# Maximum scores of two tiles in row halves of TensorE, ahead of the value products

## The chip, the cores and the metric

The kernel runs on one core of a Trainium2 chip. The metric is the device time of one execution in microseconds (us). The engines of a core run their own programs in order and wait for each other by semaphores: TensorE (PE; its weight loads are listed as PEld), VectorE (DVE), ScalarE (ACT), GpSimd (POOL) and SyncE (SP, which issues DMAs).

## The reference

Attention with normalised queries and keys (batch 8, 12 heads, 448 positions, head size 64), and behind it a mixture of eight experts with one expert a token. What the change touches is the attention:

```python
q_n, k_n = (rmsnorm(q, g_q), rmsnorm(k, g_k))
scores = scale * np.matmul(q_n, k_n.transpose(0, 1, 3, 2))
scores = scores - np.max(scores, axis=-1, keepdims=True)
attn = np.exp(scores)
attn = attn / (np.sum(attn, axis=-1, keepdims=True) + 1e-09)
return np.matmul(attn, v).astype(np.float32)
```

The maximum of a row of scores only shifts numerator and denominator of the softmax by a common factor, so it may come from less exact scores than the ones that are exponentiated.

## The kernel before

Attention goes by units: unit u is two heads of one batch entry, 48 units in all. The two heads' 896 positions make seven tiles of 128 (j = 0 to 6; tile 3 has the last 64 positions of the first head and the first 64 of the second). A unit takes seven steps; step number n = 7 i + j in the code, for n from -22 to 335. In step n TensorE makes the transposed scores of unit i, tile j (`st`, L944: a first product with 128 rows, and a second with 65, whose last row subtracts the maximum), ACT exponentiates them, and the work of other units is put around it by a plan that is written out before the loop (L1223 to L1275, from the table `PLAN`). The loop over n (L1276 on) emits each step's instructions engine by engine, so the order in the loop is the order in each engine's program. The parts that matter here:

- `tr` (L829): transposes of the normalised q or k of a unit into a PSUM tile of pool `ps_t`, which has two buffers. From it come the rounded copy `h_`, which is `hi_b[u % 2][g]` (q for g = 0, k for g = 1; the first head in partitions 0 to 63, the second in 64 to 127), and the remainder `l_` that the rounding left (function `dve`, on DVE, the last reader of the tile). DMAs move halves of both into `qq`, `kk`, `ql` and `kh`, which stack a rounded part and a remainder in 128 rows.
- `sa` (L908): scores of unit u, tile j with positions of q as rows, into one of the two buffers of pool `ps_a`; DVE reduces them to one maximum a row (`t["mx"]`). Except for unit 0 and tile 3 it multiplies `qq` by `kk`, 128 rows. For unit 0 it multiplies the rounded copies of the tile's head, 64 rows. Tile 3 multiplies the rounded copies over 128 rows with the other head's places zeroed.
- `mt` (L931): a transpose of the seven maxima of a unit into a `ps_t` buffer; ACT copies it and a DMA puts it into row 64 of `ql`.
- `av` (L982): the value products. For c = 0 to 2 they use 64 of the array's columns for each head (twelve instructions a unit, as each product of full precision is two); for c = 3, once in two units, 64 rows and 64 columns.
- `sums` (L1004), `psums` (L1013) and `gates` (L1022): products into 32 columns each (tile pm). `recips` (L1034): transposes `sp` into a `ps_t` buffer, once in four units, at step 6 behind the transposes of k.

In steady state the plan has `sa` of unit u, tile j at n = 7 u - 14 + j: each step has one `sa`, of the unit two ahead of the one in `st`. `mt` of unit u stands at n = 7 u - 6 and the value products of c = 0 to 2 at n = 7 i + 1 or so: both in step 1. The transposes of k come in step 6, those of q in step 2. In a step TensorE's order is `st`, `sa`, `tr`, `mt`, `recips`, then `av`, `sums`, `gates`. Units below 10 have times of their own in `PLAN["first"]`, and units 1 to 6 a shorter distance between their `sa` (`sastep`).

Of the kernel before, what the change touches and what calls it, by code (L numbers as in the profile page):

```python
# [69 lines left out]
def kernel(  # L70
# [660 lines left out]
    if True:  # L731
        zt = view(yw, 0, 128, NE * NT * 2 // 128)
# [543 lines left out]
        for n in range(P["start"], NJ * NU):  # L1276
            i, j = divmod(n, NJ)
# [372 lines left out]
```

## Time and profile before

| | |
|---|---|
| median of 3 runs | 1020.1 us (1019.49 to 1020.82) |
| the profiled execution | 1020.89 us, its span 1019.1 us |
| mean granted TensorE clock | 0.992 of full speed |
| PE busy | 990.7 us (97%), 5731 instructions |
| DVE, ACT, POOL busy | 797.5, 733.4, 712.9 us |
| attention stage | until some 530 us, the experts from there on |

The span is that of the instructions on the engines; the execution's time has a little around it. Busy time of matmuls is modelled (they are pipelined), so it says less than the order in which they start. Times of instructions are counted from the span's start.

### The profile page before, as it was taken

The page shows a single profiled execution, that of the slowest core. Times are in us where ns is not written, and L with a number is a line of the kernel's source. Part 1 is how long each engine was busy: PE and PEld are TensorE (multiplying, and loading weights), DVE is VectorE, ACT ScalarE, POOL GpSimd, SP SyncE. Part 2 cuts the span into 40 slices and gives each one's busy share as a digit, 9 for nine tenths or more (in the row PEclk, how much of TensorE's full clock was granted, in tenths as well). Part 3 has the DMA queues.
Part 4 walks back from the last instruction along what each step waited for, and adds up shares of the span by engine and source line. Part 5 has one row for each costly group of instructions (what it writes and reads, how often), then busy time and mean ns, then how long its engine had stood idle before and what let it go on. Part 6 is the DMA issues. An engine that isn't in the chain of part 4 may idle for free.

```text
span 1019.1 us, 18323 instructions
## 1 busy us (share of the span) xinstructions
PE 990.7 (97%) x5731; PEld 763.2 (75%) x5731; DVE 797.5 (78%) x1560; ACT 733.4 (72%) x1576; POOL 712.9 (70%) x732
## 2 busy tenths in 40 slices
PE   8999999999999999999999999999999999999996
PEld 6755656565666655555549999989999999999986
DVE  7898888887888888988569988767877777777760
ACT  8798989988989889887565566556656665666550
POOL 5767777988888989798876767566555765566141
PEclk8999999999999999999999999999999999999998
DMA  7777777777877777765753122112171211121070
GB/s 193 177 201 195 195 182 184 185 173 180 197 178 192 179 178 178 190 142 128 200 170 88 50 37 75 36 49 64 48 279 49 64 50 36 43 63 48 16 282 35
DMA packets 174430, 132.77 MB, mean 130 GB/s; under 512 B 119039, under 2 KB 168035, under 8 KB 173172
## 3 DMA queue, kind: packets, MB, share of 16 engines
q1 hardware_dynamic: 149844, 90.21, 36.8%
q0 software_dynamic: 23856, 41.28, 12.5%
q8 instruction: 47, 0.77, 0.3%
q14 instruction: 59, 0.48, 0.2%
q10 hardware_dynamic: 624, 0.02, 0.0%
HBM read 139.06 MB, written 23.72 MB: 160 GB/s over the span
## 4 chain that ended last, share of the span: by engine, by line
PE 87%; ACT 4%; DVE 4%; DMA 2%; issue 2%; POOL 1%; SPq 0%; POOLq 0%; DVEq 0%; ACTq 0%
PE py L610 23%; PE st L950 15%; PE av L994 12%; PE sa L923 5%; PE tr L836 3%; PE ph_2a L579 3%; PE ph_3s L579 2%; PE ph_0a L579 2%; PE ph_3a L579 2%; PE ph_1s L579 2%; PE ph_0s L579 2%; PE ph_1a L579 2%; PE ph_2s L579 2%; PE pm L1009 2%; DVE at_hlw L55 1%
## 5 line engine op out<-in xcount | busy, mean ns | idle before, releaser
L55 DVE TENSOR_REDUCE at_hlw<-sa 128x1 f32<-128x448 f32 x336 | 203.6, 612 | 63.8 <-PE sa L923 50.7
L950 PE MATMUL st<-w1w 128*128 128x448 f32 x480 | 174.1, 411 | 6.9 <-ACT at_w2lw L55 5.4
L55 POOL DMA_INDIRECT xrw<-x_d,i x112 | 133.5, 1192 | 33.4 <-issue 31.7
L950 PEld LDWEIGHTS st<-w1w 128*128 128x128 f32 x480 | 83.3, 189 | 97.9 <-ACT xw L55 25.6
L55 POOL DMA_INDIRECT r2w<-in_moe_w_dram,tb_w2i x48 | 50.4, 1050 | 106.0 <-DVE w2lw L55 97.3
L55 DVE TENSOR_TENSOR w1w<-r,w1w 128x512 fp32r<-128x512 f32 (+1 forms) x180 | 107.0, 644 | 14.8 <-ACT w1w L55 14.6
L55 ACT ACTIVATE at_w2lw<-st 128x448 f32<-128x448 f32 x168 | 90.0, 540 | 35.7 <-PE st L950 33.1
L610 PE MATMUL py<-w2lw,hhw 128*128 128x384 f32 x448 | 115.2, 334 | 0.0
L55 ACT CAST w1w<-xw 64x448 fp32r<-64x448 f32 x188 | 105.5, 561 | 7.0 <-DVE xw L55 3.2
L923 PE MATMUL sa<-w1w 128*128 128x448 f32 x282 | 105.5, 376 | 3.0 <-DVE at_hlw L55 2.7
L55 ACT CAST w1w<-r 128x512 fp32r<-128x512 f32 (+1 forms) x180 | 101.5, 631 | 2.0 <-DMA r<-in_moe_w_dram,ta_w1i 1.2
L55 ACT ACTIVATE r2w<-st 128x448 f32<-128x448 f32 x168 | 89.9, 539 | 16.2 <-PE st L950 10.5
L950 PE MATMUL st<-w1w,w2ha 65*128 65x448 f32 x288 | 100.3, 369 | 1.0 <-DMA w1w<-xw 1.0
L55 POOL TENSOR_TENSOR r2w<-r2w 128x448 f32<-128x448 f32 (+1 forms) x69 | 79.6, 1155 | 28.6 <-ACT r2w L55 13.5
L55 POOL TENSOR_TENSOR xrw<-r,at_hlw 112x512 f32<-112x512 f32 x85 | 90.1, 1061 | 1.2
L55 ACT ACTIVATE hhw<-yw 128x512 fp32r<-128x512 f32 x48 | 30.4, 632 | 82.1 <-DVE yw L55 82.1
L610 PEld LDWEIGHTS py<-w2lw,hhw 128*128 128x128 f32 x448 | 81.0, 188 | 0.0
L55 POOL TENSOR_TENSOR r2w<-r2w,at_w2lw 64x448 f32<-64x448 f32 (+1 forms) x46 | 53.5, 1167 | 28.3 <-DVE r2w L55 17.1
L55 ACT ACTIVATE xrw<-r 112x512 f32<-112x512 f32 (+1 forms) x154 | 68.4, 445 | 2.7 <-DMA r<-in_q_dram 1.9
L55 DVE TENSOR_TENSOR w2lw<-r2w,w2ha 128x1536 fp32r<-128x1536 f32 x28 | 49.2, 1759 | 24.4 <-ACT w2ha L55 24.4
L923 PEld LDWEIGHTS sa<-w1w 128*128 128x128 f32 x282 | 53.4, 190 | 13.5 <-DVE at_hlw L55 7.9
L55 DVE TENSOR_TENSOR w2lw<-r2w,w2hb 128x1536 fp32r<-128x1536 f32 x28 | 49.1, 1758 | 15.6 <-ACT w2hb L55 15.6
(355 smaller groups left out, 2564.2 us busy)
## 6 DMA issues: line engine op xcount, KB each, us to landing
w1w<-xw SPq DMA_DIRECT2D x312, 112.0 KB
r<-in_q_dram SPq DMA_DIRECT2D x48, 224.0 KB
r<-in_k_dram SPq DMA_DIRECT2D x48, 224.0 KB
w2ha<-xw SPq DMA_DIRECT2D x72, 112.0 KB
x_d<-at_w2hb SPq DMA_DIRECT2D x32, 168.0 KB
x_d<-yw SPq DMA_DIRECT2D x32, 168.0 KB
r2w<-in_v_dram SPq DMA_DIRECT2D x21, 128.0 KB
at_w2lw<-in_v_dram SPq DMA_DIRECT2D x19, 128.0 KB
```

The source lines that it names most:

```text
L55: return fn(*a, **kw)
L579: PE.matmul(o, lhsT=lt_, rhs=rt_, start=c == 0 and n == 0, stop=c == 5 and n == 1)
L610: PE.matmul(ps[n][:, :384], lhsT=lt_[:, j, 128 * t : 128 * t + 128], rhs=rt_[:, 384 * n : 384 * n + 384], start=j == 0 and m == 0, stop=j ...
L836: PE.transpose(sp[:, c], src[:, c], idn[:CP, :CP])
L923: PE.matmul(ps[:, :S], lhsT=t["qq"][:, h, a : a + 128], rhs=t["kk"][h], start=True, stop=True)
L950: PE.matmul(ps[:, :S], lhsT=l, rhs=t["qq"][:, h] if first else t["ql"][:, h], start=first and (j != 3 or h == 0), stop=not first and (j != ...
L994: PE.matmul(t["av"][o : o + 64, :S], lhsT=vv[r, u_ % 3, j], rhs=t["p"][r, j], start=c == (0, 3)[u_ % 2], stop=c == (3, 2)[u_ % 2])
L1009: PE.matmul(R[g][32 * i : 32 * i + 32, :S], lhsT=sel[m], rhs=T[u + i // 2]["cs"][:, i % 2 ^ i // 2], start=m == 0, stop=False, tile_positi ...
```

## The change

In each unit from 1 on, the maximum scores of tiles 1 and 5 are made from the rounded copies of q and k alone, as unit 0 does it for all: tile 1 (first head) with rows 0 to 63 of the array, tile 5 (second head) with rows 64 to 127. Both stand at place 1 of the unit's seven (`spo`), tile 0 takes the place of tile 5, and place 0 is empty. Both are emitted not with the step's other `sa`, but behind its `tr`, `mt`, `recips` and `xt`, right ahead of `av`. In steady state they stand in step 1.

```diff
-PLAN = {'pah': (1, 4), ...
+PLAN = {'sp': (1, 5), 'spo': (5, 1, 2, 3, 4, 1, 6), 'pah': (1, 4), ...
@@ sa
-            if j == 0:
-                t["mx"] = mx_b[u % 2]
+            t.setdefault("mx", mx_b[u % 2])
...
-                if u < PLAN["early"]:
+                if u < PLAN["early"] or j in PLAN["sp"]:
                     PE.matmul(ps[:, :S], lhsT=hi_b[u % 2][0][r, a : a + 128], rhs=hi_b[u % 2][1][r],
                               start=True, stop=True)
@@ the plan
                 jj = (0, 1, 2, 4, 5, 6, 3)[j] if u < P["early"] else j
-                put(when("sa", u) + int(j * P["sastep"].get(u, 1)), "sa", u, jj)
+                pj_ = j if u < P["early"] else P["spo"][j]
+                put(when("sa", u) + int(pj_ * P["sastep"].get(u, 1)), "sa", u, jj)
@@ the loop over n
             ex = st(i, ORD[i % 2][j]) if 0 <= i < NU else None
-            sm = [sa(*a) for a in todo.get("sa", ())]
+            two_ = [a for a in todo.get("sa", ()) if a[0] >= P["early"] and a[1] in P["sp"]]
+            sm = [sa(*a) for a in todo.get("sa", ()) if a not in two_]
...
                 at(pre["V"], n + 1, part(xt, *a))
+            sm += [sa(*a) for a in two_]
             for u, c in todo.get("av", ()):
                 av(u, c)
```

`early` is 1. The list `sm` holds the reductions on DVE that follow.

## Rows read from the trace of the kernel before

**Rows 1.** Sums by stretch: start:end, length, each engine's busy time, clock, DMA share.

```profile
60.00:500.00 440.00, 429.64 (x2383) 260.97 (x2381) 366.22 (x800) 380.63 (x853) 367.43 (x387) 1.00 0.73 179
```

**Rows 2.** Chain that ended last, in order of time: start, length, what.

```profile
86.86 3.56 DMA r<-in_k_dram
...
136.64 0.41 PE st L950 x2
137.05 0.20 PE sa L923
...
137.97 2.40 PE av L994 x12
140.38 0.61 PE st L950 x2
```

**Rows 3.** Timeline of TensorE, 517 to 520 us: start, length, instruction, rows*columns used.

```profile
517.63 0.54 PE L994 MATMUL av<-at_w2lw 64*64 64x448 f32 x2
518.10 0.95 PE L1019 MATMUL pm<-r2w,selw 128*32 128x448 f32 x4
518.98 0.67 PE L950 MATMUL st<-w1w 128*128 128x448 f32 x2
519.58 0.56 PE L1019 MATMUL pm<-r2w,selw 128*32 128x448 f32 x1
```

**Rows 4.** Timeline of weight loads, one at 302 and two at 517 us.

```profile
302.51 0.19 PEld L923 LDWEIGHTS sa<-w1w 128*128 128x128 f32 x1
...
517.18 0.14 PEld L994 LDWEIGHTS av<-r2w,at_w2lw 64*64 64x64 f32 x2 [0.31 <-issue]
```

**Rows 5.** Timeline of unit 0's maximum scores; a narrower stretch shows the first alone.

```profile
15.57 0.29 PEld L920 LDWEIGHTS sa<-xw 64*128 64x128 f32 x2
15.57 0.53 PE L920 MATMUL sa<-xw 64*128 64x448 f32 x1
17.12 0.74 PE L920 MATMUL sa<-xw 64*128 64x448 f32 x1
17.12 0.96 PE L920 MATMUL sa<-xw 64*128 64x448 f32 x2
19.48 1.11 PE L920 MATMUL sa<-xw 64*128 64x448 f32 x2
```

**Rows 6.** Sums by stretch around them; the granted clock is the third number from last.

```profile
15.00:15.90 0.90, 0.90 (x7) 0.74 (x6) 0.68 (x1) 0.89 (x3) 0.90 (x1) 0.96 0.90 214
...
16.50:26.00 9.50, 9.50 (x37) 8.03 (x38) 7.29 (x13) 8.20 (x54) 3.66 (x9) 0.50 0.67 162
```

**Rows 7.** Tile mt, its engines' idle time ahead of its instructions: us, times.

```profile
  DVE xw L55: 3.0, 10
```

**Rows 8.** Timeline around mt of unit 11, DVE and TensorE.

```profile
136.94 0.68 DVE L55 SCALAR_TENSOR_TENSOR xw<-tr,gs,xw 128x448 fp32r<-128x448 f32 x1
137.71 0.27 PE L934 MATMUL mt<-idn,at_hlw 128*7 128x128 f32 x1
137.91 0.60 PE L994 MATMUL av<-at_w2lw 128*64 128x448 f32 x2
```

**Rows 9.** Timeline around mt of unit 19, DVE and TensorE.

```profile
217.85 0.67 DVE L55 SCALAR_TENSOR_TENSOR xw<-tr,gs,xw 128x448 fp32r<-128x448 f32 x1
218.57 0.28 PE L934 MATMUL mt<-idn,at_hlw 128*7 128x128 f32 x1
```

**Rows 10.** Timeline around mt of unit 13, DVE and TensorE.

```profile
156.34 0.61 DVE L55 TENSOR_REDUCE at_hlw<-sa 128x1 f32<-128x448 f32 x1
157.31 0.27 PE L934 MATMUL mt<-idn,at_hlw 128*7 128x128 f32 x1
```

**Rows 11.** Timeline around mt of unit 41, DVE and TensorE.

```profile
441.49 0.61 DVE L55 TENSOR_REDUCE at_hlw<-sa 128x1 f32<-128x448 f32 x1
442.47 0.27 PE L934 MATMUL mt<-idn,at_hlw 128*7 128x128 f32 x1
```

**Rows 12.** Chain that ended last, around 422 us.

```profile
422.58 2.25 DVE at_hlw L55 x4
```

More of the change, by code (lines that the diff above doesn't have):

```diff
@@ L34 @@
 ET = mybir.EngineType
-PLAN = {'pah': (1, 4), 'vm': (40, 1), 's1n': 11, 's1r': 1.15, 'mA': (), 'lA': (), 'pj': (2, 4, 6, 5, 2, 3, 4), 'rtj': 5, 'rushat': 37, 'pe': 't', 'ave': (8, 8, 8, 8), 'avo': (15, 15, 15), 'av3': 9, 'ord': (3, 0, 1, 5, 4, 2, 6), 'xt': (10, 17), 'sm': 4, 'la': 4, 'rc': 6, 'csv': (1,), 'csj': (4, 5), 'csd': (1, 0), 'cse': (2, 2), 'sa': 14, 'mt': 6, 'tk': 22, 'tq': 19, 'nq': 29, 'nk': 25, 'sk': 49, 'sq': 50, 'rs': 46, 'ld': 58, 'first': {('sq', 0): -22, ('sk', 0): -22, ('nk', 0): -20, ('nq', 0): -20, ('sq', 1): -21, ('sk', 1): -20, ('sq', 2): -20, ('sk', 2): -18, ('nk', 1): -16, ('nq', 1): -14, ('tk', 0): -17, ('tq', 0): -18, ('sa', 0): -14, ('tk', 1): -15, ('tq', 1): -13, ('sa', 1): -3, ('mt', 0): -5, ('tk', 2): -8, ('tq', 2): -4, ('nq', 2): -8, ('nk', 2): -14, ('nq', 3): -7, ('nk', 3): -4, ('sq', 3): -14, ('sk', 3): -12, ('sq', 4): -10, ('sk', 4): -13, ('sq', 6): -5, ('sk', 6): 7, ('sk', 7): -4, ('sq', 8): 6, ('sk', 8): 9, ('nk', 7): 18, ('nq', 9): 36, ('tq', 3): 0, ('mt', 1): 1, ('nq', 5): 11, ('mt', 8): 49, ('nq', 8): 35, ('mt', 2): 10, ('nq', 7): 20, ('mt', 5): 28, ('sk', 9): 14, ('tk', 9): 41, ('mt', 6): 36, ('nq', 6): 14, ('sa', 5): 20, ('mt', 4): 20, ('nk', 4): -4, ('ld', 9): 9, ('tk', 5): 12, ('tk', 3): 3, ('tk', 4): 6, ('tq', 4): 11, ('ld', 1): -22, ('ld', 2): -22, ('ld', 3): -17, ('ld', 4): -20, ('ld', 5): -20, ('tk', 8): 33, ('sa', 3): 7, ('mt', 3): 16, ('tq', 8): 37, ('nk', 9): 39, ('ld', 6): -15, ('nk', 5): 8, ('sa', 2): 2, ('sq', 5): -16, ('tk', 7): 28, ('tq', 7): 30, ('nq', 4): 2, ('sa', 7): 35, ('tk', 6): 20, ('sq', 9): 12, ('nk', 6): 14, ('sa', 6): 28, ('tq', 9): 44, ('nk', 8): 25, ('sk', 5): -10, ('tq', 5): 14, ('ld', 8): -3, ('sq', 7): -1, ('ld', 7): -10, ('tq', 6): 22, ('rs', 8): 11, ('rs', 5): -7, ('rs', 0): -21, ('rs', 1): -18, ('rs', 2): -16}, 'rs0': {8: 0, 5: 0, 0: 0, 1: 1, 2: 2}, 'sastep': {3: 1, 4: 0.7, 1: 0.5, 2: 0.5, 0: 0.5, 6: 1, 5: 1}, 'start': -22, 'warm': {5: 8, -6: 13, -18: 0, -17: 2, -19: 0, 4: 0, 3: 0, -5: 0, -22: 3, -11: 2, -4: 2, -20: 0, -3: 0, 0: 2, 9: 0, -16: 0, 6: 0, -2: 0, -7: 0, 1: 0, 2: 0, 7: 0, -14: 3, -1: 1, 11: 0, -21: 5, 10: 0, -12: 0, -15: 4, -8: 0, -10: 1, -13: 0, -9: 0}, 'warmn': 1, 'early': 1, 'late0': 1, 'pmp0': 2, 'ramp': 10, 'pmp': (0, 0, 1, 0, 0, 1, 0), 'nv': [(0, 0), (1, 1), (2, 0), (3, 0), (5, 0), (6, 0), (7, 0), (7, 1), (8, 0), (8, 1), (9, 0)], 'pmpa': (0, 0, 1, 1, 0, 1, 1), 'rush': (-1, 1, 2), 'ps': [(0, 0), (2, 0), (3, 0), (3, 1), (5, 1), (6, 0), (7, 0), (7, 1), (9, 0)], 'pa': [(0, 0), (2, 0), (3, 1), (4, 1), (5, 1), (6, 0), (6, 1), (9, 0), (9, 1)], 'rtr': 4, 'sml': 5, 'vs': [(0, 1), (2, 1), (4, 0), (7, 0), (8, 0), (9, 1)], 'vr': [(0, 8)], 'va': [(1, 0), (1, 1), (2, 1), (3, 0), (3, 1), (4, 1), (5, 0), (5, 1), (7, 0), (7, 1)], 'ma': [], 'gain': -22, 'lv0': -4, 'lv1': -11, 'lg': ((1, -23), (1, -23), (1, -23), (0, -18), (0, -18), (0, -18)), 'lz': (9, 14, 14, 17), 'parts': {(0, 1): (1, 7, 8, 4), (0, 0): (3, 5, 3, 4), (1, 1): (0, 6, 11, 7), (2, 1): (0, 2, 7, 2), (3, 0): (2, 4, 2, 9), (1, 0): (1, 7, 5, 6), (5, 0): (0, 7, 2, 6), (4, 1): (1, 2, 5, 7), (8, 1): (2, 5, 4, 3), (7, 0): (1, 3, 5, 3), (5, 1): (1, 9, 5, 2), (6, 1): (0, 6, 2, 0), (7, 1): (0, 0, 4, 5), (3, 1): (0, 4, 3, 2), (8, 0): (0, 5, 3, 4), (2, 0): (0, 6, 6, 2), (4, 0): (0, 1, 1, 1), (6, 0): (0, 0, 3, 1), (9, 1): (0, 1, 5, 0), (9, 0): (0, 2, 0, 0)}, 'w10': (22, 18, 15), 'x0': 28, 'xr': (0, 1, 4), 'xrd': 2, 'pdef': ((0, 1, 2, 0), (0, 1, 3, 0)), 'nvd': (), 'gc': -15, 'kh': (-20, -6, -10, 2), 'zt': 4, 'pg': (5, 3), 'f1': 21, 'x1': (325, 326, 327, 328, 327, 329, 330, 332), 'gl': (33, 31, 14, 12, 10, 9, 8, 7, 6, 5), 'xs': (1, 3, 5, 6), 'wide': 2}
@@ new lines @@
+PLAN = {'sp': (1, 5), 'spo': (5, 1, 2, 3, 4, 1, 6), 'pah': (1, 4), 'vm': (40, 1), 's1n': 11, 's1r': 1.15, 'mA': (), 'lA': (), 'pj': (2, 4, 6, 5, 2, 3, 4), 'rtj': 5, 'rushat': 37, 'pe': 't', 'ave': (8, 8, 8, 8), 'avo': (15, 15, 15), 'av3': 9, 'ord': (3, 0, 1, 5, 4, 2, 6), 'xt': (10, 17), 'sm': 4, 'la': 4, 'rc': 6, 'csv': (1,), 'csj': (4, 5), 'csd': (1, 0), 'cse': (2, 2), 'sa': 14, 'mt': 6, 'tk': 22, 'tq': 19, 'nq': 29, 'nk': 25, 'sk': 49, 'sq': 50, 'rs': 46, 'ld': 58, 'first': {('sq', 0): -22, ('sk', 0): -22, ('nk', 0): -20, ('nq', 0): -20, ('sq', 1): -21, ('sk', 1): -20, ('sq', 2): -20, ('sk', 2): -18, ('nk', 1): -16, ('nq', 1): -14, ('tk', 0): -17, ('tq', 0): -18, ('sa', 0): -14, ('tk', 1): -15, ('tq', 1): -13, ('sa', 1): -3, ('mt', 0): -5, ('tk', 2): -8, ('tq', 2): -4, ('nq', 2): -8, ('nk', 2): -14, ('nq', 3): -7, ('nk', 3): -4, ('sq', 3): -14, ('sk', 3): -12, ('sq', 4): -10, ('sk', 4): -13, ('sq', 6): -5, ('sk', 6): 7, ('sk', 7): -4, ('sq', 8): 6, ('sk', 8): 9, ('nk', 7): 18, ('nq', 9): 36, ('tq', 3): 0, ('mt', 1): 1, ('nq', 5): 11, ('mt', 8): 49, ('nq', 8): 35, ('mt', 2): 10, ('nq', 7): 20, ('mt', 5): 28, ('sk', 9): 14, ('tk', 9): 41, ('mt', 6): 36, ('nq', 6): 14, ('sa', 5): 20, ('mt', 4): 20, ('nk', 4): -4, ('ld', 9): 9, ('tk', 5): 12, ('tk', 3): 3, ('tk', 4): 6, ('tq', 4): 11, ('ld', 1): -22, ('ld', 2): -22, ('ld', 3): -17, ('ld', 4): -20, ('ld', 5): -20, ('tk', 8): 33, ('sa', 3): 7, ('mt', 3): 16, ('tq', 8): 37, ('nk', 9): 39, ('ld', 6): -15, ('nk', 5): 8, ('sa', 2): 2, ('sq', 5): -16, ('tk', 7): 28, ('tq', 7): 30, ('nq', 4): 2, ('sa', 7): 35, ('tk', 6): 20, ('sq', 9): 12, ('nk', 6): 14, ('sa', 6): 28, ('tq', 9): 44, ('nk', 8): 25, ('sk', 5): -10, ('tq', 5): 14, ('ld', 8): -3, ('sq', 7): -1, ('ld', 7): -10, ('tq', 6): 22, ('rs', 8): 11, ('rs', 5): -7, ('rs', 0): -21, ('rs', 1): -18, ('rs', 2): -16}, 'rs0': {8: 0, 5: 0, 0: 0, 1: 1, 2: 2}, 'sastep': {3: 1, 4: 0.7, 1: 0.5, 2: 0.5, 0: 0.5, 6: 1, 5: 1}, 'start': -22, 'warm': {5: 8, -6: 13, -18: 0, -17: 2, -19: 0, 4: 0, 3: 0, -5: 0, -22: 3, -11: 2, -4: 2, -20: 0, -3: 0, 0: 2, 9: 0, -16: 0, 6: 0, -2: 0, -7: 0, 1: 0, 2: 0, 7: 0, -14: 3, -1: 1, 11: 0, -21: 5, 10: 0, -12: 0, -15: 4, -8: 0, -10: 1, -13: 0, -9: 0}, 'warmn': 1, 'early': 1, 'late0': 1, 'pmp0': 2, 'ramp': 10, 'pmp': (0, 0, 1, 0, 0, 1, 0), 'nv': [(0, 0), (1, 1), (2, 0), (3, 0), (5, 0), (6, 0), (7, 0), (7, 1), (8, 0), (8, 1), (9, 0)], 'pmpa': (0, 0, 1, 1, 0, 1, 1), 'rush': (-1, 1, 2), 'ps': [(0, 0), (2, 0), (3, 0), (3, 1), (5, 1), (6, 0), (7, 0), (7, 1), (9, 0)], 'pa': [(0, 0), (2, 0), (3, 1), (4, 1), (5, 1), (6, 0), (6, 1), (9, 0), (9, 1)], 'rtr': 4, 'sml': 5, 'vs': [(0, 1), (2, 1), (4, 0), (7, 0), (8, 0), (9, 1)], 'vr': [(0, 8)], 'va': [(1, 0), (1, 1), (2, 1), (3, 0), (3, 1), (4, 1), (5, 0), (5, 1), (7, 0), (7, 1)], 'ma': [], 'gain': -22, 'lv0': -4, 'lv1': -11, 'lg': ((1, -23), (1, -23), (1, -23), (0, -18), (0, -18), (0, -18)), 'lz': (9, 14, 14, 17), 'parts': {(0, 1): (1, 7, 8, 4), (0, 0): (3, 5, 3, 4), (1, 1): (0, 6, 11, 7), (2, 1): (0, 2, 7, 2), (3, 0): (2, 4, 2, 9), (1, 0): (1, 7, 5, 6), (5, 0): (0, 7, 2, 6), (4, 1): (1, 2, 5, 7), (8, 1): (2, 5, 4, 3), (7, 0): (1, 3, 5, 3), (5, 1): (1, 9, 5, 2), (6, 1): (0, 6, 2, 0), (7, 1): (0, 0, 4, 5), (3, 1): (0, 4, 3, 2), (8, 0): (0, 5, 3, 4), (2, 0): (0, 6, 6, 2), (4, 0): (0, 1, 1, 1), (6, 0): (0, 0, 3, 1), (9, 1): (0, 1, 5, 0), (9, 0): (0, 2, 0, 0)}, 'w10': (22, 18, 15), 'x0': 28, 'xr': (0, 1, 4), 'xrd': 2, 'pdef': ((0, 1, 2, 0), (0, 1, 3, 0)), 'nvd': (), 'gc': -15, 'kh': (-20, -6, -10, 2), 'zt': 4, 'pg': (5, 3), 'f1': 21, 'x1': (325, 326, 327, 328, 327, 329, 330, 332), 'gl': (33, 31, 14, 12, 10, 9, 8, 7, 6, 5), 'xs': (1, 3, 5, 6), 'wide': 2}
```

## The prediction

> **What bounds the kernel now.** I read the sums by stretch first. From 60 to 500 us, the attention stage, TensorE is busy 429.6 of 440 us at a granted clock of 1.00, which is the 2.4 GHz level; DVE is at 366, ACT at 381 and POOL at 367 [rows 1]. Then the chain of waits that ended last: after about 93 us it is nearly only TensorE, product behind product. Two score products (st) take 0.41 us, a maximum score (sa) 0.20 to 0.21, and the twelve value products 2.40; the st pair that follows the value products takes 0.61 instead of 0.41 [rows 2]. Before 93 us the chain goes through a load of k and what waits for it [rows 2], so what the change does for units 0 to 7 is mostly hidden. From about unit 8 on, TensorE's program order is the time: what an instruction takes or waits there moves the end, and ACT and DVE follow it. I therefore count TensorE's time from the maximum scores of unit 8 to those of unit 47: 40 units.
>
> **The change, part by part.** *Removed:* per unit two full sa passes, one in step 0 and one in step 1 (now j = 1) or step 5 (j = 0 takes the place of j = 5). In line, each is 0.205 [rows 2]; together 0.41.
>
> *Added:* one visit of the array in row halves in step 1, between the maximum's transpose (mt) and the value products, which run in column halves. Nothing in the trace shows this very switch. The nearest rows are switches between other shapes: the last value product in 64x64 quarters starts at 517.63, the sums in 128x32 start at 518.10, 0.47 later [rows 3]. Such products otherwise follow each other by about 0.38 (six pairs in 2.40 [rows 2]), so also a switch between two tiled shapes costs about 0.09 and then the load that nothing covers. The next rows price a whole visit: two full st products between two groups of 128x32 sums take from 518.98 to 519.58, 0.60 [rows 3]. Of that the second is 0.205, so a visit with one pass costs 0.395. I take that for the pair, because the halves seem to run side by side: two loads in quarters of the array take 0.14 together [rows 4], and unit 0, which already uses halves, ran opposite halves in 0.96 and equal halves in 1.11, one alone 0.74, at half clock [rows 5, 6]; the second of the opposite pair ended 0.22 after the first, not 0.37, and its start was late behind a PSUM buffer. That a half streams at the full rate, not at the half rate of the value products, the first one shows: 0.53 where the clock fell under way, against 0.74 [rows 5, 6]. Bounds: one pass with no switch, 0.205; halves one after the other, 0.395 plus 0.10 for a second load in line (two of the same half take 0.29 [rows 5], one load 0.19 [rows 4]) and 0.19 for a second stream, 0.685. I take 0.395, nearest to the rows of a visit.
>
> So the pair as such saves 0.41 - 0.395 = 0.015 a unit, 0.6 us in 40.
>
> The Trainium skill (TensorE: Matmul & The Clock Gate, Part 3) gives packed products the span of one plus some 4 ns for each further tile and charges nothing for the switch; by it the pair would be about 0.21, the saving 0.20 a unit and 8.0 us in all. The Trainium skill (TensorEngine Tiling (Array Packing), Key Properties) also says that a change of tiling mode, though not of tile, drains the engine; by that the 0.395 stands, and the rows of visits bear it out.
>
> *Moved:* mt of the next unit stands in step 1. Until now sa of step 0 and sa of step 1 ran ahead of it; afterwards neither does, so TensorE comes to mt 0.41 earlier, and the pair and the value products are queued behind it. mt waits for two things, both on DVE. The first is a PSUM buffer of two: in each fourth unit the gate transposes (sp) come between, and the buffer is that of k's transpose of step 6, which DVE's subtraction (xw from tr, gs) reads last. The instructions of mt waited for DVE xw ten times [rows 7]. At 137 us that subtraction ends at 136.94 + 0.68 = 137.62 and mt starts at 137.71, with 0.05 for the signal: 0.04 to spare [rows 8]. At 218 us it ends at 218.52 and mt starts 0.05 later: it waits already [rows 9]. The subtraction follows from k's transpose and its copy on ACT, which the change leaves where they are. So in these ten units mt can't start earlier, and the 0.41 of sa that used to pass meanwhile now comes after it: 0.37 to 0.41 each, mean 0.39, sum 3.9 us. The second is DVE's reduction of the unit's last sa. In nine further units it ends after TensorE's new arrival. The first: it ends at 156.95; mt, which stood at 157.31 and would be reached at 156.90 or before, could start at 157.00, and the value products at 157.00 + 0.20 + 0.395 = 157.60 instead of 157.31 + 0.20 = 157.51 (mt to value products is 0.20 [rows 8]): 0.09 late, or 0.10 beside the pair's gain [rows 10]. The last: ends 442.10, mt 442.15 instead of 442.47: 0.08 late [rows 11]. Nine times 0.1 is 0.9 us. In the other units the reduction is done in time.
>
> *At nothing:* DVE has as many reductions as before; the two of the pair fall into the 2.40 us of value products, in which TensorE brings it no other, and the two PSUM buffers that the pair needs are those of reductions that mt has waited for or that came before. The pair needs no data that came by DMA (it reads the rounded copies themselves), and j = 0 and j = 2 need theirs later than before; no DMA is added or moved past another. ACT's exponentials of step 6 must be done when step 1's st comes 0.2 earlier; I take it that they are, since the transposes of step 6 and all of step 0 lie between; if not, it costs up to 0.2 a unit.
>
> *Hidden again:* around 422 us DVE is on the chain for some microseconds [rows 12]; the one mt of the ten that lies there costs nothing more: -0.4.
>
> **Sum:** -0.6 + 3.9 + 0.9 - 0.4 = +3.8 us. The profiled execution took 1020.9 us (span 1019.1) and would take 1024.7; the median of the runs lies 0.8 lower, so I predict 1023.9.
>
> **Rivals.** (1) *The row halves cost no switch:* the visit is 0.205 instead of 0.395, 0.19 a unit, 7.6 us less: 1016.3, faster. Were it only the 0.09 between the two tiled shapes, 3.6 us less would give 1020.3, no change; it decides once the pair saves over 0.11 a unit (the other 4.4 us / 40). Against it stands the 0.47 between two tiled shapes [rows 3]; for it, that no row shows this very pair of shapes. The first rule of the Trainium skill above would make the time come out so. (2) *mt doesn't wait:* the buffer or the reduction is ready earlier, because DVE has one reduction less in step 0. Then only the pair is left: 1019.5. Against it: the subtraction stands ahead of step 0 in DVE's order. (3) *The halves don't overlap* and the change does not what it says: 0.10 (loads in line) to 0.29 a unit (loads and streams): 4 to 11.6 us more, 1027.9 to 1035.5. The quarters' loads and unit 0 speak against it.
>
> **How the numbers follow.** Forecast 0.62 (its own range 1022 to 1026.5), rival 1 0.13, rival 2 0.15, rival 3 0.10. Two tenths of a per cent, about 2 us, is what a measurement of this kernel tells from no change. Faster: rival 1, 0.13. Same: rival 2 and the lowest 0.04 of the forecast, 0.19. Slower: the rest, 0.68. The range reaches to the near ends of rivals 1 and 3, where the pair gains 0.16 or loses 0.09 a unit: 1018.0 to 1028.0.
>
> **What would show it.** Right: the half products of unit 1 and later start within 0.02 us of each other; from mt to the first value product it is about 0.6 where it was 0.20, and step 0 goes from st to st; mt's idle time for DVE xw rises from 3.0 us by about 4 in the same ten units; DVE, ACT and POOL keep their busy time. Wrong: value products that start less than 0.3 after the pair (rival 1), mt without more idle time (rival 2), half products that start 0.1 or more apart (rival 3), or new waits of st for ACT in step 1, which I cost at nothing.

## Result and profile after

The changed kernel took 1034.07 us (median of four executions, 1031.56 to 1034.87); the kernel before took 1019.8 in the same comparison (1018.63 to 1020.82). The ratio is 1.0129, with an interval of 1.0116 to 1.0142: 14.3 us slower. I had forecast 3.8 us more and a range up to 1028.0. The direction was right, the size was not: the result lies above the range.

Read the sums by stretch first. The row that answers to [rows 1] has TensorE busy for 422.2 us, where it was 429.6: 7.4 us more of the stretch are idle. Three stretches of 5 us follow in which the granted clock (third number from last) lies between its two levels; in the kernel before it is 1.00 in all three:

```profile
60.00:500.00 440.00, 422.24 (x2324) 248.43 (x2322) 361.36 (x788) 373.94 (x837) 355.91 (x377) 0.99 0.71 173
...
55.00:60.00 5.00, 4.54 (x15) 2.25 (x17) 5.00 (x8) 4.93 (x29) 4.94 (x5) 0.74 0.85 223
...
70.00:75.00 5.00, 4.30 (x15) 1.97 (x17) 2.92 (x6) 1.93 (x5) 1.61 (x2) 0.66 0.74 205
...
95.00:100.00 5.00, 5.00 (x19) 2.01 (x17) 1.71 (x4) 0.35 (x1) 1.22 (x5) 0.67 0.46 118
```

To see where the time goes, take the start of the first score product (`st`) of a unit from the two traces:

| unit | before, us | after, us | after - before | added since the row above |
|---|---|---|---|---|
| 3 | 65.31 | 67.01 | 1.70 | |
| 5 | 84.59 | 90.42 | 5.83 | 4.13 |
| 6 | 96.35 | 105.45 | 9.10 | 3.27 |
| 8 | 115.96 | 125.87 | 9.91 | 0.81 |
| 9 | 125.52 | 136.67 | 11.15 | 1.23 |
| 45 | 493.01 | 507.67 | 14.66 | 3.52 |
| 47 | 512.72 | 527.11 | 14.39 | -0.28 |

The long stretch from unit 9 to unit 45, where I had looked for nearly all of it, adds 3.52 us. Eleven lie ahead of unit 9, and those are single events. Of the 1.70 up to unit 3 little belongs to the change: in the twelve kernels below this product started between 63.91 and 66.29, the earliest in filled_36, which is the changed kernel up to there. The 0.81 hold the first of mt's waits, that of unit 7 (0.47 at 106.98).

**Units 9 to 45 go as forecast in their main term.** TensorE around mt of unit 11 ([rows 8] before), then mt of unit 19 and DVE's subtraction ahead of it ([rows 9] before):

```profile
148.21 0.36 PE L949 MATMUL st<-w1w,w2ha 65*128 65x448 f32 x1
148.80 0.28 PE L933 MATMUL mt<-idn,at_hlw 128*7 128x128 f32 x1 [0.22 <-DVE xw L55]
149.00 0.47 PE L919 MATMUL sa<-xw 64*128 64x448 f32 x2
149.41 2.48 PE L993 MATMUL av<-at_w2lw 128*64 128x448 f32 x12
...
230.47 0.28 PE L933 MATMUL mt<-idn,at_hlw 128*7 128x128 f32 x1 [0.59 <-DVE xw L55]
```

```profile
229.75 0.67 DVE L55 SCALAR_TENSOR_TENSOR xw<-tr,gs,xw 128x448 fp32r<-128x448 f32 x1
```

The pair starts 0.20 behind mt and the value products 0.41 behind the pair's start. mt waits where it was expected to: the subtraction ends at 230.42, mt starts 0.05 later and has stood idle for 0.59. Tile mt's idle time, all engines ([rows 7] before: 3.0 us, 10 times), and TensorE's own waits between 107 and 500 us:

```profile
  DVE xw L55: 12.8, 20
```

```profile
PE mt L933 <- DVE xw L55: 4.5, 10, 1.2
...
PE mt L933 <- DVE at_hlw L55: 2.1, 3, 0.9
PE sa L922 <- DVE p L56: 1.2, 1, 1.2
```

The first view counts weight loads and products alike (20 times); the second has the products alone: 4.5 us in ten of them, against 0.2 in one before. Nine of the ten are the mt of units 11, 15 and so on to 43, one in four; the tenth is that of unit 7, ahead of this stretch.

What the waits cost is read from the distance between the first score products of two units that follow each other. Around eight of the nine mt it grew by 0.38 to 0.43 us, around that of unit 39 (at 421.60 before) by 0.15: 3.35 us together. The other 27 distances add 0.17. The 2.1 us that mt waited for reductions are among those 27 and cost nothing that shows there: in units 22 and 34 it waited 0.95 and 0.93 us, but the kernel before had waited for DVE in the same places, one product earlier, and the two distances changed by 0.01 and 0.00. The product ahead of mt of unit 22, before:

```profile
248.53 0.47 PE L923 MATMUL sa<-w1w 128*128 128x448 f32 x1 [0.76 <-DVE at_hlw L55]
```

**Step 22, 3.9 us.** The score products of unit 3's first and third tile started 4.58 us apart before and 8.51 after. TensorE and DVE of the changed kernel:

```profile
68.00 0.47 PE L919 MATMUL sa<-xw 64*128 64x448 f32 x2
68.40 0.68 PE L949 MATMUL st<-w1w 128*128 128x448 f32 x2
70.70 0.48 PE L922 MATMUL sa<-w1w 128*128 128x448 f32 x1 [1.62 <-DVE at_hlw L55]
...
71.86 3.74 PE L993 MATMUL av<-r2w 128*64 128x448 f32 x12
75.52 0.68 PE L949 MATMUL st<-w1w 128*128 128x448 f32 x2
```

```profile
68.56 0.96 DVE L55 TENSOR_TENSOR xrw<-r,at_hlw 112x512 f32<-112x512 f32 x1
69.44 0.67 DVE L55 TENSOR_REDUCE at_hlw<-xrw 112x8 f32<-112x512 f32 x1
70.04 1.14 DVE L55 TENSOR_REDUCE at_hlw<-sa 128x1 f32<-128x448 f32 x2
```

The pair at 68.00 is that of unit 5. It stands in step 21 and has no value products behind it. It fills both buffers of `ps_a`; the next maximum score comes in the next step, needs one, and DVE works on the normalisation of other units until 70.04. Then the clock falls, and the twelve value products take 3.74 us instead of 2.48.

**Step 36, 4.2 us.** TensorE and ACT of the changed kernel, then the same mt and value products of the kernel before:

```profile
91.70 0.27 PE L933 MATMUL mt<-idn,at_hlw 128*7 128x128 f32 x1
91.90 0.47 PE L919 MATMUL sa<-xw 64*128 64x448 f32 x2
94.83 4.17 PE L993 MATMUL av<-r2w,at_w2lw 128*64 128x448 f32 x12 [2.45 <-ACT xw L55]
```

```profile
94.53 0.24 ACT L55 CAST xw<-mt 7x128 fp32r<-7x128 f32 x1
```

```profile
86.33 0.27 PE L934 MATMUL mt<-idn,at_hlw 128*7 128x128 f32 x1
86.54 2.48 PE L994 MATMUL av<-r2w,at_w2lw 128*64 128x448 f32 x12
```

```profile
88.71 0.24 ACT L55 CAST xw<-mt 7x128 fp32r<-7x128 f32 x1
```

The value products of unit 4 wait until ACT has copied mt, from 94.53 to 94.77. The copy's place is not new: in the kernel before ACT came to it 2.38 us behind mt (88.71, the last row; 2.83 here), but nothing waited for it. Nothing in the kernel's text asks for the wait. Which of the two `ps_t` buffers a tile gets is settled when the program is built: in the program before, these products got the other buffer, that of k's transpose, and started 0.21 us behind mt; in the changed one they got the buffer of the mt right ahead of them, and wait for its reader. The built programs have it so: mt of unit 6 and these products lie in one PSUM bank in the changed kernel and in all_but_5 and behind_36 below, and in two in the kernel before and in all_but_7.

**Step 60, 1.2 us.** DVE of the changed kernel, and the operation that answers to the last row in the kernel before:

```profile
129.33 1.15 DVE L55 TENSOR_REDUCE at_hlw<-sa 128x1 f32<-128x448 f32 x2
130.40 2.75 DVE L56 SCALAR_TENSOR_TENSOR i_w<-qf,i_w 128x1 f32<-128x1 f32 x1
133.07 0.61 DVE L55 TENSOR_REDUCE at_hlw<-sa 128x1 f32<-128x448 f32 x1
```

```profile
119.95 0.15 DVE L56 SCALAR_TENSOR_TENSOR i_w<-qf,i_w 128x1 f32<-128x1 f32 x1
```

An operation on one column of numbers takes 2.75 us instead of 0.15, and the reduction behind it keeps a `ps_a` buffer that TensorE waits for 1.2 us (`PE sa <- DVE p` above; the view names the small operation next to the reduction, but the reduction ends at 133.68 and TensorE's product starts at 133.73). The section on the hardware comes back to it.

### The profile page after: what moved, and what is told of

It reads as the page before. It is cut to its first block, busy times and chain, and to the rows that moved or that the text cites. A ratio compares the mean times of both kernels' runs of the same rounds, so it can differ in the third digit from the quotient of the medians.

```text
span 1033.1 us, 18324 instructions
## 1 busy us (share of the span) xinstructions
PE 996.5 (96%) x5731; PEld 756.5 (73%) x5731; DVE 800.5 (77%) x1560; ACT 733.2 (71%) x1576; POOL 713.1 (69%) x732
## 5 line engine op out<-in xcount | busy, mean ns | idle before, releaser
L55 DVE TENSOR_REDUCE at_hlw<-sa 128x1 f32<-128x448 f32 x336 | 200.3, 612 | 62.0 <-PE sa L922 41.9
L922 PE MATMUL sa<-w1w 128*128 128x448 f32 x188 | 71.0, 379 | 4.7 <-DVE at_hlw L55 1.9
L55 DVE TENSOR_REDUCE at_hlw<-xrw 112x8 f32<-112x512 f32 x84 | 56.0, 678 | 14.9 <-ACT xrw L55 14.8
```

What stands on the lines that cost most here:

```text
L55: return fn(*a, **kw)
```

## The experiments

Twelve kernels, run on three chips, on which the kernel before took 1053.82, 1020.35 and 1035.76 us (medians). Where two kernels do the same, the short stretches of the attention stage agree between the chips to some hundredths of a us at full clock (to 0.3 where the clock falls: 3.93 and 3.64 in unit 3), and units 9 to 45 to 0.36 (3.40 to 3.76); the rest of a run does not. So each kernel is compared with the kernel before by its ratio on its own chip, and by stretches of the attention stage in its trace. The table gives what each stretch takes more than in the kernel before (us, from starts of score products): from the first to the third tile of unit 3 (4.58 before) and of unit 5 (4.35), unit 8 (9.57), and units 9 to 45 (367.49).

| kernel | ratio to before, interval | unit 3 | unit 5 | unit 8 | 9 to 45 |
|---|---|---|---|---|---|
| changed | 1.0129, 1.0116 to 1.0142 | 3.93 | 4.15 | 1.23 | 3.52 |
| pair_from_8 | 1.0086, 1.0060 to 1.0111 | 0.02 | 0.01 | 1.27 | 3.76 |
| pair_beside | 1.0110, 1.0083 to 1.0137 | 0.00 | 4.15 | 1.27 | 3.71 |
| pair_ahead_of_mt | 1.0042, 1.0012 to 1.0072 | 0.02 | 0.01 | 1.27 | 2.01 |
| order_full | 1.0067, 1.0040 to 1.0095 | 0.00 | 0.01 | 1.28 | 4.52 |
| all_but_7 | 1.0098, 1.0077 to 1.0119 | 3.93 | -0.01 | 1.27 | 3.40 |
| pair_twice | 1.0098, 1.0080 to 1.0117 | 0.02 | 0.02 | 1.29 | 8.72 |
| mt_behind | 0.9983, 0.9974 to 0.9993 | 0.00 | 0.01 | 1.28 | -3.25 |
| before_mt_behind | 0.9963, 0.9951 to 0.9975 | 0.00 | 0.01 | 0.02 | -3.65 |
| all_but_5 | 1.0090, 1.0056 to 1.0124 | 0.00 | 2.45 | 1.25 | 3.52 |
| filled_36 | 1.0084, 1.0051 to 1.0118 | 3.64 | 2.46 | 1.24 | 3.43 |
| behind_36 | one execution | 3.92 | 4.46 | 1.26 | 3.42 |
| pair_from_11 | 0.9951, 0.9924 to 0.9978 | 0.00 | 0.01 | 0.03 | -3.12 |

Which units have the pair is set by one line in each kernel, and three places ask it:

```diff
+PAIRED = lambda u: u >= 8
-                if u < PLAN["early"] or j in PLAN["sp"]:
+                if u < PLAN["early"] or PAIRED(u) and j in PLAN["sp"]:
-                pj_ = j if u < P["early"] else P["spo"][j]
+                pj_ = P["spo"][j] if PAIRED(u) else j
-            two_ = [a for a in todo.get("sa", ()) if a[0] >= P["early"] and a[1] in P["sp"]]
+            two_ = [a for a in todo.get("sa", ()) if PAIRED(a[0]) and a[1] in P["sp"]]
```

**pair_from_8** (the lines above). 

> The pair only for units 8 and up; units 1 to 7 keep their maximum scores as before the change. Theory A (the opening): the value stage pays what the prediction said for mt's early arrival, and the rest of the loss comes from units 1 to 7. In the changed kernel the first score product of unit 9 is 11.1 us later than before and that of unit 47 14.4 us, so 3.3 to 4 us belong to the steady part: 1023 to 1024 us, and the three stretches of half clock between 57 and 98 us are gone. Theory B (the pair itself is dear, or row halves make the clock fall where they first come up): the loss moves with the pair, 1030 us or more, with new half-clock stretches behind unit 8.

Units 3 and 5 are back to the times of before, and the clock is 1.00 from 55 to 100 us; units 9 to 45 add 3.76, as in the changed kernel. Theory A holds for these two events. The 1.27 in unit 8 stay, so that event is not the opening's. The total is a miss: 1.0086 is 9 us more than before, at least 6 by the interval, where I had expected 3.3 to 4. The attention stage shows some 5 of them; where the rest lies stays open. (On this chip the kernel before alone spread over 12 us.)

**pair_beside** (`PAIRED = lambda u: u > 0 and u not in (1, 2, 4, 5)`). 

> The pair for all units but 0, 1, 2, 4 and 5, those whose pair does not stand beside value products. Theory A: without value products behind the pair its two reductions hold both ps_a buffers, and the next maximum score waits; with the four units as before, the lag of 5.6 us that the changed kernel had by unit 3, place 2 is gone, the 4.4 us at unit 5, place 2 stay: about 1028.5 us. Rival (a late ACT or the clock alone, not these pairs): 1034, with the 3.7 us value products of step 22 still there. Second rival (the two jumps have one cause, and the second goes with the first): 1024.

Unit 3's 3.93 are gone, unit 5's 4.15 stay to the hundredth: two events, and the second doesn't need the first.

**all_but_5** (`PAIRED = lambda u: u > 0 and u != 5`). 

> The pair for all units but 0 and 5. The pair of unit 5 stands in step 21, with no value products behind it; in the changed kernel the next maximum score (step 22) waited 1.62 us for DVE, and the value products behind it took 3.74 us instead of 2.48. Theory A (that pair holds both ps_a buffers while DVE is busy with the normalising of other units): wait and half clock of step 22 are gone, the last mt 3 to 3.6 us earlier than the 519.5 of the changed kernel, step 36 unchanged. Rival (it takes the pairs of units 1, 2 and 4 too): the wait stays, 519.5.

Step 22 is unit 5's pair: without it, though the pairs of units 1, 2 and 4 stay, there is no wait, and the value products there take 2.48 us. Step 36 keeps its wait but costs 2.45 instead of 4.15, which I had not expected. TensorE in step 36:

```profile
87.24 0.47 PE L920 MATMUL sa<-xw 64*128 64x448 f32 x2
90.16 2.48 PE L994 MATMUL av<-r2w,at_w2lw 128*64 128x448 f32 x12 [2.45 <-ACT xw L56]
```

The wait is the same 2.45 us and the clock does not fall. (The last mt came at 513.1, where I had expected some 516.)

**all_but_7** (`PAIRED = lambda u: u > 0 and u != 7`). 

> The pair for all units but 0 and 7. The pair of unit 7 stands in step 36, beside the value products of unit 4, which in the changed kernel waited 2.45 us for ACT's copy of mt and then took 4.17 us instead of 2.48. Without it the value products of unit 4 get the other ps_t buffer (that of k's transpose, as before the change) and not mt's own. Theory A (that wait is the shared buffer): no wait there, no half clock behind it, the last mt about 4 us earlier than in the changed kernel (515 to 516 instead of 519.5), step 22 unchanged. Rival (ACT or the clock is late there for another reason): the wait stays, the last mt at 519.

```profile
91.31 0.27 PE L934 MATMUL mt<-idn,at_hlw 128*7 128x128 f32 x1
91.58 2.48 PE L994 MATMUL av<-r2w,at_w2lw 128*64 128x448 f32 x12
```

No wait, value products at full clock, unit 5 as before, unit 3 unchanged; the last mt at 515.0. The other buffer and the missing pair come together here, and the next kernel parts them.

**behind_36.** 

> The changed kernel, with the pair of unit 7 behind the value products of step 36 instead of ahead of them; the value products of unit 4 keep the ps_t buffer of mt. Theory A (the shared buffer): the wait for ACT's copy of mt stays, 2.4 to 2.9 us, half clock behind it, last mt 519 to 520. Rival (the pair in front of them is what holds the value products up, and all_but_7 helped because it left the pair out): no wait, last mt at 515.

```diff
-            sm += [sa(*a) for a in two_]
+            if n != 36:
+                sm += [sa(*a) for a in two_]
...
+            if n == 36:
+                sm += [sa(*a) for a in two_]
             for a in todo.get("sums", ()):
```

```profile
88.90 0.27 PE L933 MATMUL mt<-idn,at_hlw 128*7 128x128 f32 x1
92.00 4.08 PE L993 MATMUL av<-r2w,at_w2lw 128*64 128x448 f32 x12 [2.83 <-ACT xw L55]
```

With nothing between mt and the value products, but in mt's buffer, they wait 2.83 us for its copy. It is the buffer, not the pair in front of them, by this one execution. (The last mt came at 517.3, since this execution started 2.8 us earlier at unit 3.)

**filled_36** (the halves of the pair of step 36 are issued eleven times more). 

> The changed kernel, with the pair of step 36 made eleven times more, 2.2 us of products in the 2.45 us in which TensorE waited there for ACT's copy of mt. Theory A (the wait is ACT's, and the longer value products are the half clock behind an idle TensorE): the value products start at the same time, 2.9 us behind the pair's start, but take 2.48 us and not 4.17; the last mt 1.5 to 1.7 us earlier, 518. Rival 1 (the clock falls for another reason): 4.17 as before, 519.5. Rival 2 (TensorE's work, not ACT, sets their start): 2.2 us later, 521.7.

```diff
             sm += [sa(*a) for a in two_]
+            for u_, j_ in two_ * (11 if n == 36 else 0):
+                T[u_]["again", j_]()
```

```profile
88.50 0.47 PE L919 MATMUL sa<-xw 64*128 64x448 f32 x2
88.81 2.39 PE L921 MATMUL sa<-xw 64*128 64x448 f32 x22
91.44 2.48 PE L995 MATMUL av<-r2w,at_w2lw 128*64 128x448 f32 x12 [0.24 <-ACT xw L55]
```

The value products start 2.94 us behind the pair, as in the changed kernel (2.93), and take 2.48: the wait is ACT's, and what comes on top is the clock. That an idle TensorE made it fall is not shown by this alone, since all_but_5 was idle as long and kept its clock. (The last mt came at 514.3 and not at 518; 3.1 us of the 5.2 to the changed kernel's 519.5 were there at unit 3 already.)

**order_full** (as pair_from_8, with `if u < PLAN["early"]:` in `sa`, so the pair is two products of 128 rows). 

> As pair_from_8 in order, but the two products of the pair are full ones of 128 rows from qq and kk, no row halves. Theory A (the place counts, the row halves save about nothing): 0.41 instead of 0.398 us a unit, so within 1 us of pair_from_8, 1023 to 1025 us. Rival (the row halves and their switches are the loss, the place is free): 1020 us, as before.

4.52 against 3.76 in units 9 to 45: the loss comes with the place, not with the row halves, which save some 0.02 a unit.

**pair_ahead_of_mt.** 

> As pair_from_8, but the pair stands ahead of mt instead of behind it: mt then comes at its old time, less 0.015 us. Theory A (what the steady part loses is mt's waits): the 3.3 to 4 us are gone, 1019 to 1020 us, mt's idle time for DVE near that of before (3.0 and 2.2 us). Rival (the pair costs more in line than the two products it replaces, or its switches do): one more change of shapes a unit, st, pair, mt, av, at 0.09 to 0.19 us, 3.6 to 7.6 us in 40 units: 1023 to 1027 us.

```diff
             sm = [sa(*a) for a in todo.get("sa", ()) if a not in two_]
+            sm += [sa(*a) for a in two_]
...
-            sm += [sa(*a) for a in two_]
             for u, c in todo.get("av", ()):
```

```profile
158.35 0.37 PE L950 MATMUL st<-w1w,w2ha 65*128 65x448 f32 x1
158.66 0.47 PE L920 MATMUL sa<-xw 64*128 64x448 f32 x2
159.06 0.28 PE L934 MATMUL mt<-idn,at_hlw 128*7 128x128 f32 x1
159.26 0.97 PE L994 MATMUL av<-at_w2lw 128*64 128x448 f32 x4
```

Between the two theories: TensorE's waits for DVE at mt are 0.9 us in all, as before (0.8), but units 9 to 45 take 2.01 us more, where the forecast for the pair alone is 0.5 less. From the last st to the value products it takes 0.91 (0.31, 0.40, 0.20), and in the changed kernel's order 0.81 (0.21, 0.20, 0.40, where mt doesn't wait): a further change of shapes costs 0.1 a unit, and 2.5 of its 3.6 us show. They lie where mt's waits did not: the nine units of those waits add 0.18, the other 27 add 1.83.

**pair_twice.** 

> As pair_from_8, but the two half products are made twice (first, second, first, second). From the pair's start to the value products it took 0.398 us. If that is one pass at full rate (0.205) and 0.19 for the visit, the second pass adds 0.19 to 0.21 us a unit, 8 us in 40 units: last mt at 518 instead of 510.2. If the halves share a rate and the visit is free, it adds 0.40 a unit: last mt at 526. If the pair hides beside other work, it adds nothing: 510.

```diff
             sm += [sa(*a) for a in two_]
+            for u_, j_ in two_:
+                T[u_]["again", j_]()
```

```profile
159.84 0.47 PE L920 MATMUL sa<-xw 64*128 64x448 f32 x2
160.15 0.36 PE L922 MATMUL sa<-xw 64*128 64x448 f32 x2
160.44 2.09 PE L996 MATMUL av<-at_w2lw 128*64 128x448 f32 x9
```

0.60 from the pair's start to the value products instead of 0.40: a second pass of both halves costs 0.20, so they do run side by side, and the visit itself costs the other 0.20. In units 9 to 45 it shows 4.96 of 7.2 us (8.72 against 3.76); the last mt came at 516.8.

**mt_behind.** 

> As pair_from_8, but mt of units 8 and up stands behind the value products of its step instead of ahead of the pair. Theory A (the steady part's loss is mt's waits for DVE, 22.5 us idle in pair_from_8 against 5.2 before): mt's inputs are 2.8 us older when TensorE comes to it, so nearly all of that idle time goes and the attention stage ends 3 us or more before that of before: first score products of the last units some 9 us earlier than in pair_from_8, the whole 0.99 to 1.00 of before. Rival (the pair and its switches are the loss): 5 us later than before, as pair_from_8. Second rival (the maximum then reaches ql too late, and st waits for its DMA instead): idle time of st for DMA, time as pair_from_8 or later.

```diff
-            for a in todo.get("mt", ()):
+            for a in todo.get("mt", ()) if n < 50 else ():
                 at(pre["A"], n + 1, mt(*a))
...
+            for a in todo.get("mt", ()) if n >= 50 else ():
+                at(pre["A"], n + 1, mt(*a))
             for a in todo.get("sums", ()):
```

**before_mt_behind** (the same edit in the kernel before). 

> The kernel before the change, no pair, with mt of units 8 and up behind the value products. Theory A: mt's 5.2 us of idle time for DVE go, so up to 5 us less than before, and mt_behind differs from this by what the pair itself does (0.6 us less to 1.5 us more). Rival: mt's wait only covers another that comes right behind it, and nothing is gained: within 1 us of before.

Both gain: 7.0 us in units 9 to 45 against pair_from_8 (I had expected 9), and 3.65 against before. TensorE of before_mt_behind:

```profile
146.18 2.48 PE L994 MATMUL av<-r2w,at_w2lw 128*64 128x448 f32 x12
148.58 0.28 PE L934 MATMUL mt<-idn,at_hlw 128*7 128x128 f32 x1
148.61 0.66 PE L950 MATMUL st<-w1w 128*128 128x448 f32 x2
```

mt takes 0.03 in line behind the value products, where it took 0.20 ahead of them [rows 8], and it no longer waits for DVE. Unit by unit, the 27 without that wait gain 0.07 us each, 1.89 together, and the nine with it 1.76: an estimate from these is 2.5 us for the place in line and 1.1 for the wait. So Theory A, which had only the wait, held for the smaller part. With the pair (mt_behind) the same stretch is only 0.40 longer: in this place the pair costs what it saves.

**pair_from_11** (as mt_behind, `PAIRED = lambda u: u >= 11`). 

> As mt_behind, but the pair only for units 11 and up. In mt_behind a scalar operation of the routing on DVE took 2.77 us at step 60 while POOL was busy without a gap (0.15 before), and TensorE waited 1.24 us for the reduction behind it. Theory A (the pair itself costs what it saves; what mt_behind still lost against before_mt_behind is this one operation, which the pairs of units 9 and 10 move on DVE, and the start): 0 to 1 us above before_mt_behind, 0.996 to 0.998 of before, the operation back at 0.2 us. Rival (the pair costs in every unit): 2.4 us above, 0.998 to 0.999 of before.

```profile
119.99 0.15 DVE L57 SCALAR_TENSOR_TENSOR i_w<-qf,i_w 128x1 f32<-128x1 f32 x1
```

The small operation takes 0.15 again, and unit 8 loses 0.03 instead of 1.28. So that event belongs to the pairs of units 8 to 10. 0.9951 and 0.9963 (before_mt_behind) can't be told apart; both beat the two kernels of the case.

## Why the prediction was wrong, step by step

- **The step that failed** stands in the first part: "Before 93 us the chain goes through a load of k ..., so what the change does for units 0 to 7 is mostly hidden." The chain of before showed what bounds that stretch while nothing else is late. It did not show how much later something else may come. Two waits took 1.62 and 2.45 us there, the value products behind them 1.3 and 1.7 us more, in part at half clock: with what stands around them 8.1 us (3.93 and 4.15), of which 0.9 came back by unit 6.
- **"At nothing" failed with it.** "The two of the pair fall into the 2.40 us of value products" holds for steady state. The places of units 1, 2, 4 and 5 come from the table of exceptions and have no value products behind them; for unit 5 that was the 3.93 us (all_but_5).
- **No step asked which buffer a tile would get.** I took from the trace of before which PSUM buffer mt would wait for, and that held in the nine units. Unit 4's value products got another one (all_but_7, behind_36).
- **No step looked at POOL.** The pairs of units 8 to 10 move DVE's small operation by under a microsecond, to where POOL works without a gap: 1.2 us.
- **The pair's cost was right:** 0.395 forecast, 0.40 measured, halves together, 0.20 of it the visit (pair_twice). The Trainium skill (TensorE: Matmul & The Clock Gate, Part 3) would have it at about 0.21; the trace does not agree for the visit (0.40), but does for a further pass (0.20). The Trainium skill (TensorEngine Tiling (Array Packing), Key Properties) has a change of tiling mode drain the engine; the 0.20 a visit and the 0.1 in pair_ahead_of_mt go with that.
- **mt's early arrival was right in its main term:** for the wait for DVE's subtraction the forecast was 3.9 less 0.4 us, at 0.39 a unit; 3.35 were measured, 0.40 a unit in eight units and 0.15 in the one at 422 us. The ten waits that I read as ten units [rows 7] were nine units, with weight load and product of unit 43 both counted. The reductions were mis-sized: 0.9 us forecast, next to nothing measured, and in the two units that it was worked out for, 13 and 41, the change was 0.01 and -0.02. The pair's saving of 0.6 did not show either. So 3.52 against 3.4 (the forecast's 3.8 for 40 units, taken for these 36) is right in the main term and luck in the rest, where two small misses cancel.
- **Rivals.** Rival 1 (no cost of a switch) and rival 3 (no overlap) fall with pair_twice, rival 2 (mt doesn't wait) with mt's rows. None of them had an event in the opening, and the range took its upper end from rival 3 alone.

## What to carry to other kernels

A change that repeats in every unit is costed from steady state, but its first units often stand elsewhere: list where the moved instruction falls in each of them, and for each ask which buffers it holds and who is next for them. That one chain bounds a stretch says nothing of how much slack the others have there. And a change of order can change which buffer a later tile gets: in the built program, compare which engine each instruction waits for, not only the order.

## What was unexpected in the hardware

- A DVE operation on 128x1 took 2.75 us at 130.40 instead of 0.15, while POOL went through three products without a gap:

```profile
129.98 1.04 POOL L55 TENSOR_TENSOR xrw<-r,at_hlw 112x512 f32<-112x512 f32 x1
130.98 1.15 POOL L55 TENSOR_TENSOR at_w2lw<-r2w,at_w2lw 128x448 f32<-128x448 f32 x1
132.09 1.04 POOL L55 TENSOR_TENSOR xrw<-r,at_hlw 112x512 f32<-112x512 f32 x1
133.09 2.35 POOL L55 TENSOR_TENSOR r2w<-r2w 128x448 f32<-128x448 f32 x2
```

It ended at 133.15, just behind the third. In the kernel before it came at 119.95, ahead of the first of them, and took 0.15. There the next operation of its kind came into the third and took 0.96, till just behind its end; in the changed kernel it came at 134.19, where the two products of POOL's last row leave 0.08 between them, and took 0.14. Before, DVE and POOL:

```profile
122.29 0.96 DVE L56 SCALAR_TENSOR_TENSOR p<-qf,p 128x1 f32<-128x1 f32 x1
122.19 1.04 POOL L55 TENSOR_TENSOR xrw<-r,at_hlw 112x512 f32<-112x512 f32 x1
```

The Trainium skill (SBUF — State Buffer, SBUF: two separate sides) says that a DVE operation with two inputs in SBUF and a GpSimd operation that reads SBUF exclude each other for a whole instruction. The trace agrees, and adds that the loser waited through three in a row. No run took POOL's work away, so the cause is read from these rows, not tried; pair_from_11 shows only that the pairs of units 8 to 10, which move the moment, decide.
- The same 2.45 us of idle TensorE were followed by half clock in the changed kernel (value products 4.17 us), in pair_beside (4.17) and, after 2.83 us, in behind_36 (4.08), and not in all_but_5 (2.48). What decides stays open. The stretch of half clock between 55 and 60 us came and stayed away both without a pair ahead of it (before_mt_behind 0.74, pair_from_8 1.00) and with one (changed 0.74, filled_36 1.00), so the change alone doesn't make it.
